# Raw blocks of the seven-product units side by side, x statistics partly on ScalarE, two more gate/up units made in the first quarter and down's weights later

## The chip, the cores and the metric

One NeuronCore of a Trainium2 chip runs the kernel. TensorE (PE) multiplies, VectorE (DVE), ScalarE (ACT) and GpSimd (POOL) work elementwise, and SyncE (SP) issues the DMAs, one after the other in program order. Every engine has its own queue and takes its instructions in order; an instruction whose semaphore has not come holds up all that is queued behind it on that engine. The metric is device time in microseconds (us), median of three runs.

## The reference

A block of two layers over x (2048 rows, 448 columns), each with a residual: a Fourier mixing and a gated feed-forward. All weights and transform matrices are inputs.

```python
x = A_x
h  = x + A(layernorm(x))      # a = xn @ Wd_re.T, b = xn @ Wd_im.T ; y = Ws_re @ a - Ws_im @ b
h2 = h + B(layernorm(h))      # g = hn @ w_gate, u = hn @ w_up ; (gelu(g) * u) @ w_down
# Ws: 2048 x 2048 (re, im); Wd: 448 x 448 (re, im); w_gate, w_up: 448 x 1792; w_down: 1792 x 448
```

The layer norms have no scale or shift, the gelu is the tanh approximation, and everything is float32.

## The kernel before

**Precision.** Every float32 operand is split into a high f16 part (ACT, `hi_part`, L105) and a low f16 part (DVE, `lo_part`, L108), and every product is made of three matmuls: high by high and the two cross terms.

**The transform (to about 347 us).** An F slot computes the features a and b of one tile of 128 rows; a U slot ("unit") multiplies one block of the sequence matrix with the features of a pair of tiles. Eight passes of eight units make h, 256 rows a pass; passes accumulate in four PSUM banks. Three units are plain (24 matmuls), and five, `S_UNITS`, use a scheme of seven half products (42 matmuls of half the width). Such a unit needs, besides raw blocks of its weights (`wr`), four sums of them (`seq_sums`, L515, on DVE), all split into high and low; of the four raw blocks it uses three, which are numbers 0, 2 and 3, in two instructions per engine (`seq_parts`, L525). The features of such a tile get sums too (`feature_sums`). At the same time the other engines make ready what comes later: the statistics and the norm of the next x tiles, the layer norm of finished passes, their splitting into operands of the feed-forward part and the DMA transposes of these (`ffn_sums`, `ffn_hi`, `ffn_lo`, `ffn_transpose`), and the weights of 11 of the 14 gate/up units, which are summed, split and stored to DRAM (`Weights.high`, `Weights.low`). The order of all this on each queue is made by a planner (`arranged`, L928) when the program is built: tasks with a cost, a due time and predecessors, taken by due time per engine. Due times carry an offset by kind (`SHIFT`). The order before it, from L980 to L1036, is written out by hand.

**The feed-forward part.** Four quarters of 512 rows in operands, 14 gate/up units each (t = 0 to 55; loop at L1439). A gate/up unit has seven products, 39 matmuls on three PSUM banks X, Y and Z. In the code they are `x_open`, `x_close`, `y_open`, `y_mid`, `y_close`, `z_open` and `z_close`; the part called hh is read out of Z and Y by DVE (L1209, L1266) with help of ACT (`u2`, `u3`, the gelu), and POOL multiplies its last block (`c_last`). `y_mid`'s read of Z must be over before `z_close` adds to the bank. From t = 14 on each unit is followed by 21 matmuls of the down projection for the hidden rows made earlier (`dn_mm`), with down chunk n = d mod 7 of the weights, d = t - 14.

**The first quarter (t = 0 to 13)** has no down matmuls. In it are made

- the gate/up units in `LATE` (4, 8, 12), from raw weights in the order of beats, two to a unit t (`late_prep(2 * t)` after `y_mid`, `late_prep(2 * t + 1)` at the end); a beat issues sums, high parts and low parts; one raw tile is loaded (`gu_late`) as soon as the one before is read;
- down's seven weight chunks (`down_load`, `down_sums` on POOL, `down_hi`, `down_lo`, driven by `down_prep(t - 1)`): chunk n belongs to t = 2n + 1 and 2n + 2; its raw tile `wd32` takes one of two buffers in turn, and two chunks are loaded ahead, the first already in the transform.

Work beside the units, such as the norm and splitting of pass pairs for quarters 2 and 3 and the drains of down, hangs in a table `side` and is issued by `do(t, k)` at place k of unit t; within a unit of quarters 1 to 3 the places come in the order 0, 6, 1, 4, 5, 2, 3, 7, and in quarter 0 there are none.

Of the kernel before, what the change touches and what calls it, by code (L numbers as in the profile page):

```python
# [33 lines left out]
def kernel(  # L34
# [57 lines left out]
    G.memset(eps_t, EPS / X_SC**2)  # L92

# [115 lines left out]
    def ffn_root(q, j):  # L209
        moments[q, j] = moments[q, j], root(moments[q, j], f"h{q}_{j}", moments_of(q, j))  # L210

    def ffn_rstd_steps(q, j):
        mv, sd = moments[q, j]
        found = []
        steps = rstd_steps(found, mv, sd, f"h{q}_{j}", const, moments_of(q, j))
        next(steps)
        moments[q, j] = mv, found[0]
        yield
        yield from steps
# [8 lines left out]
    def down_load(n):  # L228
        wd32[n] = fops.tile([P, 4, HD], F32, tag="tt" if n % 2 else "xn", name=f"wd32_{n}")
        nc.sync.dma_start(wd32[n].rearrange("p (k c) d -> p k (c d)", k=2), w_down[n])  # L230
# [91 lines left out]
    S_UNITS, WR_BUFS, WS_BUFS, WSS_BUFS, STAGE_BUFS = (3, 4, 5, 6, 7), 3, 3, 2, 2  # L322
    ORDER = (0, 1, 5, 2, 6, 3, 7, 4)
# [4 lines left out]
    xt, xs, xT, norm_x = {}, {}, {}, {}  # L328
    x_pairs = x.rearrange("(u g p) d -> u p g d", g=2, p=P)
# [27 lines left out]

    def x_root(*tiles):
        norm_x[tiles] = norm_x[tiles], root(norm_x[tiles], f"x{tiles[0]}")

    def x_rstd_steps(*tiles):
        mv, sd = norm_x.pop(tiles)
        found = []
        steps = rstd_steps(found, mv, sd, f"x{tiles[0]}")
# [10 lines left out]
    def x_bias(*tiles):  # L375
        mv, r, _ = norm_x[tiles[0]]
        nb = small.tile([P, len(tiles)], F32, tag=f"nb{len(tiles)}", name=f"nb_x{tiles[0]}")
        bias_of(nb, mv, r)
        for i in tiles:
            norm_x[i] += (nb,)  # L380
# [134 lines left out]
    def seq_sums(p, u):  # L515
        r = wr[p, u]
        s = wsum[p, u] = dft.tile([P, 4, 2 * P], F32, tag="wsum", bufs=1, name=f"wsum{p}_{u}")
        V.tensor_add(s[:, 0:2], r[:, 1:2].to_broadcast([P, 2, 2 * P]), r[:, 0:4:3])
        yield
        V.tensor_add(s[:, 2], s[:, 1], r[:, 0])  # L520
        yield
        V.tensor_add(s[:, 3], s[:, 2], r[:, 2])  # L522
# [39 lines left out]
    PRODUCTS = [(0, 0, 2, 0), (1, 2, 0, 1), (6, 1, 0, 0), (2, 6, 1, 1), (4, 3, 2, 1), (5, 5, 3, 0), (3, 4, 3, 1)]  # L562
# [42 lines left out]
    def seq_out(p):  # L605
# [12 lines left out]
        for g, ps in enumerate((X, Y)):  # L618
            eg = e[:, 2 * g : 2 * g + 2].rearrange("p o d -> p (o d)")
# [10 lines left out]
    class Weights:  # L630
# [52 lines left out]
        def beat(self, k):  # L683
# [19 lines left out]
    for k, u in enumerate(ORDER):  # L703
        slots += [("F", i) for i in tiles_of[k]]
        due = [v for v in ready if not is_s(v) or ORDER.index(v) < k - 1]
        if k:
            slots += [("U", 0, v) for v in due[:1]]
            ready = [v for v in ready if v not in due[:1]]
# [22 lines left out]
    class Task:  # L731
# [5 lines left out]
    SHIFT = {"copy": -31.8, "fhigh": -68.2, "fhighp": -18.1, "flow": 9.9, "fsum": 12.9, "guhi": 1.2, "gulo":  # L737
        22.8, "guraw": -33.2, "gus1": -3.2, "gus2": 31.0, "hbias": -61.6, "hhi": -17.7, "hlo": 16.0,
        "hnorm": -24.0, "hroot": 35.4, "hrstd": 5.9, "hsum": 23.1, "htr": 140.0, "mom": 32.7, "out": -5.4,
        "seed": -14.0, "shigh": -55.6, "slow": 3.4, "whigh": -12.1, "whigh_s": -34.3, "wload": -73.7,  # L740
        "wlow": 2.9, "wlow_s": -3.8, "wsum": -12.5, "xbias": 12.2, "xlo": 1.3, "xnorm": 26.7, "xroot": -6.1,
        "xrstd": 21.6, "xstat": 21.3, "xturn": -1.8}
    HOLD = (0.23, 17.8)
# [6 lines left out]
    def add(*args, **kw):  # L750
        tasks.append(Task(*args, **kw))
        return tasks[-1]

    def chain(engine, costs, due, make, after=(), kind=None):
# [8 lines left out]
        for k, cost in enumerate(costs):  # L763
            last = [add(engine, cost, due, lambda k=k: step(k == 0), after=last, kind=kind)]
# [14 lines left out]
    for k, (i, i2) in enumerate(tiles_of):  # L779
        n = where["F", i]  # L780
        if k > 1:
# [4 lines left out]
            t = add("V", 1.35, T[max(n - 6, 0)] + first_pair, lambda i=i, j=i2: x_stats(i, j), begin=T[max(n - 7, 0)] - 13.0, after=[t], kind="xstat" if k > 2 else None)  # L786
            t = add("A", 0.3, T[max(n - 5, 0)] + first_pair, lambda i=i, j=i2: x_root(i, j), after=[t], kind="xroot" if k > 2 else None)
            t = chain("V", (0.2, 0.1, 0.1, 0.1), T[max(n - 5, 0)] + first_pair, lambda i=i, j=i2: x_rstd_steps(i, j), [t], kind="xrstd" if k > 2 else None)
            t = add("V", 0.15, T[max(n - 5, 0)] + first_pair, lambda i=i, j=i2: x_bias(i, j), after=[t], kind="xbias" if k > 2 else None)
            for c in (i, i2):  # L790
                n = where["F", c]
                low = fixed(n - 5, 5, "A", 1.15, lambda i=c: x_norm(i), [t], kind="xnorm")
                low = fixed(n - 5, 5, "V", 0.85, lambda i=c: x_lo(i), [low], kind="xlo")
                turned[c] = fixed(n - 4, 2, "SP", 1.3, lambda i=c: x_turn(i), [low], lag=2.6, kind="xturn")
                steps[n].after += [turned[c]]
        for c in (i, i2):
# [8 lines left out]
            else:  # L805
# [4 lines left out]
                t = drained = add("V", 1.07, T[n + 1] + 2.5 if n > 1 else -30.0 + n, lambda i=c: feature_low(i), after=[t], kind="flow" if n > 1 else None)  # L810
# [15 lines left out]
    for g, (p, u) in enumerate(units):  # L826
# [23 lines left out]
    at_end = T[len(slots)]  # L850
    h_done, rooms, last_e = {}, {}, []
    for p in range(N_PASS):
# [15 lines left out]
        t = add("A", 0.25, t0 + 14.0, lambda q=q, j=j: ffn_root(q, j), after=m, kind="hroot")  # L868
        t = chain("V", (0.2, 0.1, 0.1, 0.1), t0 + 15.0, lambda q=q, j=j: ffn_rstd_steps(q, j), [t], kind="hrstd")
        last_e, h_done[p] = m, [store, t]  # L870
        if q < 2:
            t = add("V", 0.15, t0 + 16.0, lambda q=q, j=j: ffn_bias(q, j), after=[t], kind="hbias")
            t = add("A", 1.35, t0 + 17.0, lambda q=q, j=j: ffn_norm_act(q, j, hp[q, j]), after=[t], kind="hnorm")
            h_done[p] = [store, t]
            for k in range(4):
# [12 lines left out]
    LATE = {4: 0, 8: 7, 12: 15}  # L888
# [35 lines left out]
    t = fixed(len(slots) - 14, 9, "SP", 0.1, lambda: down_load(0), last_e, lag=6.0, kind="dload")  # L924
    fixed(len(slots) - 8, 9, "G", 4.0, lambda: down_sums(0), [t], kind="dsum")
# [115 lines left out]
    for _, t in arranged():  # L1041
# [10 lines left out]
        if t == p1_end:  # L1052
            first.close()
# [31 lines left out]
    down_load(1)  # L1085
# [83 lines left out]
    def down_prep(t):  # L1169

        n, odd = divmod(t, 2)
        if odd:
            if n < NC:
                down_lo(n, 1)
                if n + 2 < NC:
                    down_load(n + 2)
            if n + 1 < NC:
                down_sums(n + 1)
        elif n < NC:
            down_hi(n, 0)  # L1180
            down_lo(n, 0)

# [142 lines left out]
    def dn_drain(p):  # L1325
        v = [ftile(f"v{k}", 1, f"v{k}_{p}", D) for k in range(2)]
# [37 lines left out]
    for q in (2, 3):  # L1364
# [53 lines left out]
    late_beats = {n + k: (f, k) for f, n in LATE.items() for k in range(6)}  # L1418
    assert len(late_beats) == 6 * len(LATE)

    def late_prep(beat):
        if beat not in late_beats:
            return
        f, k = late_beats[beat]
        gu[f].beat(k)
        after = [v for v in LATE if v > f]
        if k == 3 and after:
            gu_late(after[0])
        if k == 5:
            gw[f] = gu[f].w  # L1430
# [8 lines left out]
    for t in range(N_GU):  # L1439
# [12 lines left out]
        if d >= 0 and d % NC == 1:  # L1452
# [4 lines left out]
        if q == 0:  # L1457
# [8 lines left out]
            if t > 0 and t % 2 == 0 and t < 2 * NC:  # L1466
                down_hi(t // 2 - 1, 1)
# [5 lines left out]
            if t > 0:  # L1473
                down_prep(t - 1)
            late_prep(2 * t + 1)
        else:
# [80 lines left out]
    assert not side  # L1557
# [59 lines left out]
```

## Time and profile before

| what | value |
|---|---|
| median of 3 runs | 707.02 us (705.33 to 707.19) |
| profiled execution: span, first to last instruction | 703.5 us |
| mean granted clock of TensorE | 0.999 |
| transform | to about 347.4 us |
| first quarter | about 347.5 to 409 us |
| quarters 1 to 3 and the end | 409 to 703.5 us |
| PE, DVE, ACT, POOL busy | 697.0, 563.2, 408.0, 198.8 us |
| DMA, 16 engines | 139.74 MB, mean 199 GB/s |

The times of the table's stages are read off the timeline of PE, where the instructions change from one line of the kernel to another. Busy time of an engine is the union of its instructions; a PE instruction overlaps its neighbours, so the mean duration of a matmul is longer than the distance to the next. Where a view of the profile names a releaser, it is the event that ended an idle stretch.

### The profile page before, as it was taken

The page shows a single profiled execution, that of the slowest core. Times are in us where ns is not written, and L with a number is a line of the kernel's source. Part 1 is how long each engine was busy: PE and PEld are TensorE (multiplying, and loading weights), DVE is VectorE, ACT ScalarE, POOL GpSimd, SP SyncE. Part 2 cuts the span into 40 slices and gives each one's busy share as a digit, 9 for nine tenths or more (in the row PEclk, how much of TensorE's full clock was granted, in tenths as well). Part 3 has the DMA queues.
Part 4 walks back from the last instruction along what each step waited for, and adds up shares of the span by engine and source line. Part 5 has one row for each costly group of instructions (what it writes and reads, how often), then busy time and mean ns, then how long its engine had stood idle before and what let it go on. Part 6 is the DMA issues. An engine that isn't in the chain of part 4 may idle for free.

```text
span 703.5 us, 15378 instructions
## 1 busy us (share of the span) xinstructions
PE 697.0 (99%) x6046; PEld 584.1 (83%) x6046; DVE 563.2 (80%) x1170; ACT 408.0 (58%) x862; POOL 198.8 (28%) x225
## 2 busy tenths in 40 slices
PE   8999999999999999999999999999999999999998
PEld 5556578878787878778888889999999999999998
DVE  6999999999999897989578877575765755786786
ACT  5776674667576565656267765555555544455432
POOL 0000000000000000001136754474664745647342
PEclk9999999999999999999999999999999999999999
DMA  9554555687988867777579665658466594545401
GB/s 330 160 128 114 142 170 184 233 245 227 228 275 202 283 177 261 262 253 281 182 258 353 204 211 170 191 180 199 170 195 190 178 200 173 181 158 166 151 27 54
DMA packets 81849, 139.74 MB, mean 199 GB/s; under 512 B 41712, under 2 KB 59376, under 8 KB 81776
## 3 DMA queue, kind: packets, MB, share of 16 engines
q1 hardware_dynamic: 81776, 138.76, 63.5%
q8 instruction: 47, 0.77, 0.5%
q14 instruction: 26, 0.21, 0.1%
HBM read 109.25 MB, written 20.19 MB: 184 GB/s over the span
## 4 chain that ended last, share of the span: by engine, by line
PE 95%; DMA 1%; ACT 1%; DVE 1%; issue 1%; SPq 0%; ACTq 0%; DVEq 0%
PE acc L574 38%; PE acc_d L1144 15%; PE pY L1199 14%; PE pZ L1199 9%; PE pX L1199 9%; PE ab L457 9%; DMA x<-in_x_dram 1%; DVE dn_w L110 0%; ACT dn_w L106 0%; SPq L429 0%; ACT xn_h L254 0%; DVE st_x L354 0%; DVE hh L1209 0%; ACT wd L106 0%; ACT g L1252 0%
## 5 line engine op out<-in xcount | busy, mean ns | idle before, releaser
L1199 PEld LDWEIGHTS <-gw 128*128 128x128 f16 x2184 | 213.1, 98 | 23.7 <-issue 1.0
L574 PE MATMUL acc<-b,ws 128*128 128x224 f16 (+1 forms) x1296 | 204.6, 301 | 0.0
L574 PEld LDWEIGHTS <-ws 128*128 128x128 f16 x1296 | 125.6, 98 | 53.2
L1199 PE MATMUL pY<-hops,gw 128*128 128x256 f16 x952 | 129.1, 273 | 0.0
L1144 PE MATMUL acc_d<-wd,dn_w 128*128 128x224 f16 x1050 | 122.3, 259 | 0.0
L574 PE MATMUL acc<-b,wss 128*128 128x224 f16 x960 | 118.2, 259 | 0.0
L235 POOL TENSOR_TENSOR wd_s<-wd 128x448 f32<-128x448 f32 x7 | 10.1, 1442 | 346.8 <-DMA wr<-in_w_seq_dram 330.0
L1144 PEld LDWEIGHTS <-dn_w 128*128 128x128 f16 x1050 | 101.1, 98 | 2.9
L574 PEld LDWEIGHTS <-wss 128*128 128x128 f16 x960 | 92.3, 98 | 0.1
L106 ACT ACTIVATE ws<-wr 128x256 f16<-128x256 f32 (+2 forms) x104 | 62.4, 637 | 41.1 <-PE acc L574 16.1
L1199 PE MATMUL pZ<-hops,gw 128*128 128x256 f16 x616 | 85.5, 273 | 0.4 <-DVE hh L1209 0.3
L1276 POOL TENSOR_TENSOR hh<-hh,c 128x256 f32<-128x256 f32 x56 | 46.3, 828 | 139.7 <-ACT c L1274 139.5
L1199 PE MATMUL pX<-hops,gw 128*128 128x256 f16 x616 | 83.3, 273 | 0.0
L112 DVE SCALAR_TENSOR_TENSOR ws<-wr,ws 128x256 f16<-128x256 f32 (+2 forms) x104 | 70.6, 709 | 1.4 <-ACT ws L106 1.3
L110 DVE TENSOR_TENSOR dn_w<-hh,dn_w 128x256 f16<-128x256 f32 x50 | 25.3, 506 | 53.1 <-ACT dn_w L106 52.8
L106 ACT ACTIVATE wss<-wsum 128x1024 f16<-128x1024 f32 x40 | 42.1, 1053 | 36.8 <-DVE wsum L522 21.1
L457 PEld LDWEIGHTS <-xT 128*128 128x128 f16 x352 | 33.9, 98 | 32.8 <-ACT xT L420 1.5
L110 DVE TENSOR_TENSOR dn_w<-dn_s,dn_w 128x640 f16<-128x640 f32 x50 | 54.6, 1092 | 7.4 <-ACT dn_w L106 6.7
L1243 ACT ACTIVATE u<-pY 128x256 f32<-128x256 f32 x56 | 21.4, 382 | 61.4 <-PE pY L1199 61.3
L1291 POOL TENSOR_TENSOR dn_s<-hh 128x256 f32<-128x256 f32 x42 | 52.8, 1258 | 0.0
L112 DVE SCALAR_TENSOR_TENSOR wss<-wsum,wss 128x1024 f16<-128x1024 f32 x40 | 48.8, 1220 | 4.1 <-ACT wss L106 4.0
L1238 ACT ACTIVATE pY<-pX 128x256 f32<-128x256 f32 x56 | 20.6, 368 | 50.3 <-PE pX L1199 50.3
(120 smaller groups left out, 936.9 us busy)
## 6 DMA issues: line engine op xcount, KB each, us to landing
gw<-w_dram SPq DMA_DIRECT2D x53, 896.0 KB, 4.8
wr<-in_w_seq_dram SPq DMA_DIRECT2D x64, 512.0 KB, 4.4
gu_raw<-in_w_gu_dram SPq DMA_DIRECT2D x28, 384.0 KB, 4.8
w_dram<-gu_p SPq DMA_DIRECT2D x33, 256.0 KB, 3.1
hx<-in_x_dram SPq DMA_DIRECT2D x8, 448.0 KB, 4.5
h_dram<-hx SPq DMA_DIRECT2D x8, 448.0 KB, 4.8
hr<-h_dram SPq DMA_DIRECT2D x8, 448.0 KB, 5.3
x<-in_x_dram SPq DMA_DIRECT2D x7, 448.0 KB, 6.9
```

Of the source, the lines that this page charges most:

```text
L106: A.activation(dst, src, AF.Copy, scale=scale)
L110: V.tensor_sub(dst, src, hi)
L112: V.scalar_tensor_tensor(dst, src, scale, hi, op0=ALU.mult, op1=ALU.subtract)
L235: G.tensor_sub(s[:, 2:4], t[:, 0:2], t[:, 2:4])
L457: PE.matmul(feat[i][r][:, :D], xT[i][:, kx, :], w[:, kw, r * D : (r + 1) * D], start=n == 0, stop=n == 10,)
L574: PE.matmul(banks[k][:, cols], lhs, rhs, start=k not in begun, stop=stop, skip_group_check=True)
L1144: PE.matmul(acc[k // 2][:, k % 2 * HD : (k % 2 + 1) * HD], a_of(la, a), b_of(lb, b), start=first and m == 0 and k % 2 == 0, stop=last and ...
L1199: PE.matmul(ps, w[:, wl, wa + ws, :], ops[:, m + ms, :], start=first and n == 0, stop=last and n == len(terms) - 1, skip_group_check=True,)
L1238: A.activation(self.Y, self.X, AF.Copy)
L1243: A.activation(self.u2, self.Y, AF.Copy, scale=SC)
L1276: G.tensor_mul(c22, c22, self.c12)
L1291: E.tensor_sub(s[:, 2:4], t[:, 1:4:2], t[:, 0:4:2])
```

## The change

- *Raw blocks*: the seven-product scheme is rewritten with rows exchanged, so that it uses raw blocks 1, 2 and 3, which lie side by side; one instruction per engine splits them where there were two. `PRODUCTS` and the read-out (`seq_out`) exchange the banks accordingly.
- *Statistics*: for the x pairs 7 and 4 the sums are made by ACT (two passes with accumulation) and no longer by DVE. Where ACT makes the sums, for x or for h, two small steps of the reciprocal root go to ACT as well.
- *Slots*: a plain unit follows its features at once, a seven-product unit one pair later than before; `SHIFT` and `HOLD` have new values.
- *First quarter*: `LATE` has five units; beats are five to a unit instead of six and follow one another from 0 to 23; a raw tile is asked for at the third beat. The splitting and transposes of pass 3 (second quarter's operands) leave the transform for t = 0 to 4.
- *Down's weights*: chunk n belongs to t = 6 + 2n and 7 + 2n, to t = 19; `wd32` has one buffer (tag v, which the drains use later), loaded one chunk ahead at the end of t = 6 + 2n; the first load and its sums are at the end of t = 4 and t = 5, behind the transposes. `down_hi` of the sums goes to `down_mid`.
- *Quarter 2's splitting* is five and eight units later, but its first norm stays at t = 14; one load of h for a drain is three units later.
- SBUF: the last b tile takes the place of an x tile, so that the first pool lives to the end of the transform.

The diff, cut to its core:

```diff
+    def half_of(mv, tag, pool=small, of=1):
+        n = mv.shape[1]
+        r = pool.tile([P, 4, n], F32, tag=f"r{n}" if pool is small else f"r_{tag}", name=f"r_{tag}")
+        A.activation(r[:, 1], mv[:, :, 1], AF.Identity, scale=-0.5 / (of * X_SC**2), bias=half_eps)
+        return r
...
-        V.tensor_mul(r[:, 2], r[:, 0], r[:, 0])
+        if by_vector:
+            V.tensor_mul(r[:, 2], r[:, 0], r[:, 0])
+        else:
+            A.activation(r[:, 2], r[:, 0], AF.Square)
...
     def down_load(n):
-        wd32[n] = fops.tile([P, 4, HD], F32, tag="tt" if n % 2 else "xn", name=f"wd32_{n}")
+        wd32[n] = fpool.tile([P, 4, HD], F32, tag="v", name=f"wd32_{n}")
...
+    BY_SCALAR = (7, 4)
+    HALF, BEHIND = {}, 0
...
+    def x_moments(i, tiles):
+        if i == tiles[0]:
+            norm_x[tiles] = small.tile([P, 2, 2], F32, tag="mv2", name=f"mv_x{i}")
+        act_moments(norm_x[tiles][:, tiles.index(i), :], xt[i][0], junk)
...
-        V.tensor_add(s[:, 0:2], r[:, 1:2].to_broadcast([P, 2, 2 * P]), r[:, 0:4:3])
+        V.tensor_add(s[:, 0:2], r[:, 0:1].to_broadcast([P, 2, 2 * P]), r[:, 1:3])
...
-            return [(w[0], slice(0, 1), r[:, 0:1]), (w[0], slice(1, 3), r[:, 2:4])]
+            return [(w[0], slice(0, 3), r[:, 1:4])]
...
-            if k > 1:
-                s0, s1, src = parts[k - 2]
+            for n in ((), (), (0, 1), (2,), (3,))[k]:
+                s0, s1, src = parts[n]
                 lo_part(self.slots(1, s0, s1, src), src, self.slots(0, s0, s1, src), W_SC)
-            if 0 < k < 5:
-                s0, s1, src = parts[k - 1]
+            for n in ((), (0, 1), (2,), (3,), ())[k]:
+                s0, s1, src = parts[n]
                 hi_part(self.slots(0, s0, s1, src), src, W_SC)
...
+            if i % 2 == HALF.get(k, 1):
+                due = [v for v in ready if ORDER.index(v) < k - (2 if is_s(v) else BEHIND)]
...
-    LATE = {4: 0, 8: 7, 12: 15}
+    LATE = {4: 0, 6: 5, 9: 10, 11: 15, 13: 19}
...
-    t = fixed(len(slots) - 14, 9, "SP", 0.1, lambda: down_load(0), last_e, lag=6.0, kind="dload")
-    fixed(len(slots) - 8, 9, "G", 4.0, lambda: down_sums(0), [t], kind="dsum")
...
         n, odd = divmod(t, 2)
         if odd:
-            if n < NC:
+            if 0 <= n < NC:
                 down_lo(n, 1)
-                if n + 2 < NC:
-                    down_load(n + 2)
-            if n + 1 < NC:
+            if n + 1 < NC and n >= 0:
                 down_sums(n + 1)
-        elif n < NC:
+        elif 0 <= n < NC:
             down_hi(n, 0)
             down_lo(n, 0)
+            if n + 1 < NC:
+                down_load(n + 1)
+
+    WD0 = 6
+
+    def down_mid(t):
+        n, odd = divmod(t - WD0, 2)
+        if odd and 0 <= n < NC:
+            down_hi(n, 1)
...
+        (4, 4, lambda: ffn_transpose(1, 1, (2,))),
+        (4, 4, lambda: ffn_transpose(1, 1, (3,))),
+        (4, 4, lambda: down_load(0)),
+        (5, 4, lambda: down_sums(0)),
...
+            if k == 2 and after:
+                gu_late(after[0])
...
             late_prep(2 * t)
...
+            do(t, 1)
+            down_mid(t)
             nxt.z_open()
             nxt.y_open()
             cur.y_close()
             cur.z_close()
             dn_ahead(t)
-            if t > 0:
-                down_prep(t - 1)
+            do(t, 2)
+            down_prep(t - WD0)
             late_prep(2 * t + 1)
+            do(t, 4)
         else:
...
             if nxt:
                 nxt.y_open()
-            if t == 2 * NC:
-                down_hi(NC - 1, 1)
-            if t == 2 * NC + 1:
-                down_lo(NC - 1, 1)
+            down_mid(t)
+            down_prep(t - WD0)
             do(t, 2)
```

More of the change, by code (lines that the diff above doesn't have):

```diff
@@ L92 @@
     G.memset(eps_t, EPS / X_SC**2)
+    half_eps = const.tile([P, 1], F32, name="half_eps")
+    G.memset(half_eps, -0.5 * EPS / X_SC**2)
     warm = const.tile([P, 1], F32, name="warm")
@@ L328 @@
     xt, xs, xT, norm_x = {}, {}, {}, {}
+    by_scalar = tuple((2 * u, 2 * u + 1) for u in BY_SCALAR)
+    junk = p1.tile([P, D], F16, name="junk")
     x_pairs = x.rearrange("(u g p) d -> u p g d", g=2, p=P)
@@ L356, in x_stats, with x_of @@
             V.bn_aggr(mv[:, g, :], st)
+    def x_moments(i, tiles):
+        if i == tiles[0]:
+            norm_x[tiles] = small.tile([P, 2, 2], F32, tag="mv2", name=f"mv_x{i}")
+        act_moments(norm_x[tiles][:, tiles.index(i), :], xt[i][0], junk)
+    def x_of(tiles):
+        return D if tiles in by_scalar else 1
     def x_root(*tiles):
-        norm_x[tiles] = norm_x[tiles], root(norm_x[tiles], f"x{tiles[0]}")
+        mv, of, tag = norm_x[tiles], x_of(tiles), f"x{tiles[0]}"
+        r = half_of(mv, tag, small, of) if of > 1 else None
+        norm_x[tiles] = mv, root(mv, tag, of), r
     def x_rstd_steps(*tiles):
-        mv, sd = norm_x.pop(tiles)
+        mv, sd, r = norm_x.pop(tiles)
         found = []
-        steps = rstd_steps(found, mv, sd, f"x{tiles[0]}")
+        steps = rstd_steps(found, mv, sd, f"x{tiles[0]}", of=x_of(tiles), r=r)
         next(steps)
@@ L501, in sums_high @@
     def sums_high(i):
-        t = bop[i] = dft.tile([P, 2, 7, HD], F16, name=f"b{i}")
+        if i == tiles_of[-1][1]:
+            t = p1.tile([P, 2, 7, HD], F16, tag="xs", name=f"b{i}")
+        else:
+            t = dft.tile([P, 2, 7, HD], F16, name=f"b{i}")
+        bop[i] = t
         hi_part(t[:, 0], b32[i][:, 1:8])
@@ L703 @@
     for k, u in enumerate(ORDER):
[L704 to L708, printed above, removed]
+        for i in tiles_of[k]:
+            slots.append(("F", i))
+            if i % 2 == HALF.get(k, 1):
+                due = [v for v in ready if ORDER.index(v) < k - (2 if is_s(v) else BEHIND)]
+                slots += [("U", 0, v) for v in due[:1]]
+                ready = [v for v in ready if v not in due[:1]]
         ready.append(u)
@@ L763, in chain @@
         for k, cost in enumerate(costs):
-            last = [add(engine, cost, due, lambda k=k: step(k == 0), after=last, kind=kind)]
+            on, cost = cost if isinstance(cost, tuple) else (engine, cost)
+            last = [add(on, cost, due, lambda k=k: step(k == 0), after=last, kind=kind)]
         return last[0]
@@ L1084 @@
     h_store(N_PASS - 1)
-    down_load(1)
     banks_dft.close()
@@ L1325, in dn_drain @@
     def dn_drain(p):
-        v = [ftile(f"v{k}", 1, f"v{k}_{p}", D) for k in range(2)]
+        v = fpool.tile([P, 2, D], F32, tag="v", name=f"v_{p}")
+        v = [v[:, k] for k in range(2)]
         return Drain(hr[p], acc_d[p], v, 1.0 / (H_SC * W_SC))
@@ L1416 @@
     odd_q = None
-    late_beats = {n + k: (f, k) for f, n in LATE.items() for k in range(6)}
-    assert len(late_beats) == 6 * len(LATE)
+    late_beats = {}
+    for f, n in LATE.items():
+        for k in range(5):
+            at(late_beats, n + k, (f, k))
     def late_prep(beat):
[L1422 to L1430, printed above, removed]
+        for f, k in late_beats.pop(beat, ()):
+            gu[f].beat(k)
+            after = [v for v in LATE if v > f]
+            if k == 2 and after:
+                gu_late(after[0])
+            if k == 4:
+                gw[f] = gu[f].w
     cur = GateUp(0)
@@ L1556 @@
     part_store(7, 1, 1)
-    assert not side
+    assert not side and not late_beats
 def _tiles(inputs):
```

122 lines of the change are left out of this document (86 added, 36 removed).

## The prediction, made before the changed kernel was run

> **What bounds the kernel now.** I read the page first, then the chain of waits in order of time, then the first quarter of the feed-forward part unit by unit.
>
> ```profile
> span 703.5 us, 15378 instructions
> PE 697.0 (99%) x6046; PEld 584.1 (83%) x6046; DVE 563.2 (80%) x1170; ACT 408.0 (58%) x862; POOL 198.8 (28%) x225
> PE 95%; DMA 1%; ACT 1%; DVE 1%; issue 1%; SPq 0%; ACTq 0%; DVEq 0%
> ```
>
> A busy PE need not be at its peak, so I compare lengths in the chain (start, us, what) with counts.
>
> ```profile
> 13.37 2.44 PE ab L457 x12
> ...
> 27.77 4.54 PE acc L574 x24
> ...
> 61.82 4.03 PE acc L574 x42
> ...
> 99.38 248.30 PE acc L574 x2100
> 349.65 1.20 PE pX L1199 x11
> ...
> 672.09 28.19 PE acc_d L1144 x294
> ```
>
> A plain unit takes 4.54, a seven-product unit 4.03. The 2100 matmuls are 21 plain and 38 seven-product units: 95.3 + 153.1 = 248.5 us, and the row has 248.30. So the transform has no stall there. In the feed-forward part a gate/up matmul takes 1.20/11 = 0.109 and a down matmul 28.19/294 = 0.0959; 2184 and 1176 of them make 351.1 us. They fill 347.5 (the first gate/up matmul, 2.1 before the 349.65 row) to 672.09 + 28.19 = 700.3, which is 352.8. **All the stalls that could be won back behind 13.4 us are some 1.7 us, 0.24%.** One of them has this row:
>
> ```profile
> 420.12 0.71 PE L1199 MATMUL pZ<-hops,gw 128*128 128x256 f16 x5 [0.29 <-DVE hh L1209]
> ```
>
> Before 13.4 us the order is written out by hand, and the change leaves it alone; the tail after 700.3 too.
>
> **The change part by part, at the profiled execution's own 703.5.** The median of the runs, 707.02, is 3.5 above this span; I put that on top of the new sum.
>
> The transform first (the grouped view of 100 to 340 us, and of the whole).
>
> ```profile
> L112 DVE SCALAR_TENSOR_TENSOR ws<-wr,ws 128x512 f16<-128x512 f32 x36 | 24.6, 684 | 0.1
> L112 DVE SCALAR_TENSOR_TENSOR ws<-wr,ws 128x256 f16<-128x256 f32 x36 | 15.0, 418 | 0.3 <-ACT ws L106 0.3
> L106 ACT ACTIVATE xs<-tt 128x768 f16<-128x768 f32 x4 | 3.3, 827 | 0.0
> L354 DVE BATCH_NORM_STATS2 st_x<-x 128x6 f32<-128x448 f32 x16 | 9.2, 613 | 4.3 <-DMA x<-in_x_dram 4.3
> L128 ACT ACTIVATE e<-hx,mv_h 128x448 f32<-128x448 f32 x14 | 9.4, 669 | 0.5
> ```
>
> *Raw blocks side by side*: 40 times, DVE's 684 + 418 ns become one operation of 768 columns, bounded by 684 and 1102; by length 0.95. That is some 6 us less for DVE; ACT's one is near the 827. *Statistics*: four tiles of x lose about 0.8 each on DVE (613 and its aggregate) and gain about 1.8 each on ACT (two passes like the 669, with accumulator reads). The two small steps that each root now gives to ACT are under 0.5 us nine times. *Two gate/up units and one pass's splitting leave the transform*: DVE loses some 4.4 and 5 us apiece. All of it is worth **zero to the end**, since PE runs without a gap over this work; were the cover gone, DVE's relief, some 25 us in 330, could count. *The new slot order* keeps the same matmuls; it puts four F slots in a row at units 7 and 4. Bounds: 0, and a rival below. I take 0, by the 248.30 row.
>
> Now the first quarter (units t = 0 to 13). What matters there is PE, unit 4 here, and what DVE had:
>
> ```profile
> 366.69 1.36 PE L1199 MATMUL pX<-hops,gw 128*128 128x256 f16 x11
> ...
> 370.41 0.71 PE L1199 MATMUL pZ<-hops,gw 128*128 128x256 f16 x5
> 370.95 1.36 PE L1199 MATMUL pX<-hops,gw 128*128 128x256 f16 x11
> ```
>
> A unit lasts 4.26, so unit 10 starts at 392.2. Its z_close is 3.72 in (the pZ row), at 395.9, and cannot start until DVE's hh of that unit has read the Z bank; hh is queued behind all that DVE was given before.
>
> **The step that I expect to cost: a chain through one buffer.** The old kernel had two buffers for down's raw weights; the new one has one (tag v), and reads of it on POOL (down_sums), ACT and DVE must be over before the next load. SP issues in order, so what stands behind a waiting load waits too. Both are in the old trace:
>
> ```profile
> 376.01 1.04 POOL L238 TENSOR_TENSOR wd_s<-wd 128x224 f32<-128x224 f32 x1
> ```
> ```profile
> 375.12 0.81 SPq L637 DMA_DIRECT2D gu_raw<-in_w_gu_dram  x2
> ...
> 377.08 0.33 SPq L230 DMA_DIRECT2D wd<-in_w_down_dram  x1
> ...
> 389.36 7.66 SPq L1073 DMA_DIRECT2D gw<-w_dram  x2
> ```
>
> The load at 377.08 went when POOL's sums ended at 377.05; at 389.36 SP stood still until a tile came free. The terms (the tile views of wd, of gu_raw, both 340 to 430 us, and the line of the transposes; ns min/median/max):
>
> ```profile
> L106 ACT ACTIVATE wd<-wd_s x7: 1125/1127/1129, 361.1 to 416.0; 128x1120 f16<-128x1120 f32 x7
> L112 DVE SCALAR_TENSOR_TENSOR wd<-wd_s,wd x7: 1308/1315/1319, 363.0 to 421.4; 128x1120 f16<-128x1120 f32 x7
> L235 POOL TENSOR_TENSOR wd_s<-wd x6: 1127/1326/1518, 364.4 to 408.1; 128x448 f32<-128x448 f32 x6
> L237 POOL TENSOR_TENSOR wd_s<-wd x6: 1128/1136/1313, 365.9 to 409.2; 128x448 f32<-128x448 f32 x6
> L238 POOL TENSOR_TENSOR wd_s<-wd x6: 651/654/1048, 367.0 to 410.3; 128x224 f32<-128x224 f32 x6
> DMA to landing us min/median/max: 4.0/5.5/7.0
> ```
> ```profile
> L112 DVE SCALAR_TENSOR_TENSOR gw<-gu_raw,gw x6: 420/684/1023, 356.8 to 390.9; 128x512 f16<-128x512 f32 x3, 128x256 f16<-128x256 f32 x3
> L643 DVE TENSOR_TENSOR gu_s<-gu_raw x3: 544/548/1079, 352.8 to 385.4; 128x384 f32<-128x384 f32 x3
> DMA to landing us min/median/max: 3.1/5.0/5.9
> ```
> ```profile
> L315 SPq DMA_TRANSPOSE hops<-xs x32: 1183/1297/3398, 152.2 to 573.3; - x32
> ```
>
> Five gate/up units now share beats 0 to 23, two to a unit, and the raw tile of the next is asked for at the third beat. For unit 9 that is the end of t = 3: DVE starts there at about 367.0 (z_close of t = 3 ends as 366.69 begins), does c, a small split and two low parts (0.34 + 0.2 + 0.95), so SP issues the two loads at 368.5. Behind them on SP: those loads 0.8, two transposes 2.6, a gate/up load and a store 0.7, two transposes 2.6; down_load(0) goes at **375.2** and lands 5.5 later, 380.7. POOL sums it, 1.33 + 1.14 + 0.65 = 3.1: 383.8. Only then may down_load(1) go: lands 389.3, summed 392.4. down_load(2) goes then (0.33), and *behind it on SP* stand the two raw loads for unit 13 (second issue at 393.2): landed 398.2. DVE has the first sums of unit 13 in its queue at the end of t = 9, so it stands until 398.2, does them (0.55 + 0.3) and hh (0.42): 399.5. PE's z_close of unit 10, due at 395.9, is **3.6 us late**. On the way ACT waits for chunk 0 at the end of t = 6 and for chunk 1 at the end of t = 8, with the next unit's gelu and its copy of X into Y queued behind, and PE's y_open behind that copy. Those stalls, under 1 each, are inside the 3.6, for the chain runs through absolute times. With every minimum (4.0, 2.9, 4.0, 2.9, 3.1) unit 13's weights land at 392.9, before DVE needs them: 0. With every maximum the lateness is near 9. I take the medians, since the DMA engines are nearly full already in 362 to 389 us (packets, MB, share of 16 engines), and the change brings two gate/up loads and stores more into the quarter:
>
> ```profile
> q1 hardware_dynamic: 2004, 9.38, 94.8%
> ```
>
> The splitting of pass 3, now in t = 0 to 4, gives DVE some 0.7 a unit where down's parts (1.8 a pair of units) stood before: 0. What later weights wait for is then covered, since quarter 1's units last longer (below, 6.27).
>
> **A second one, at t = 20.** The last chunk's high and low parts are issued at the end of t = 19, behind y_open; dn_mm of t = 20 is the first to read them, in its second product term. The same place in the old trace:
>
> ```profile
> 446.03 0.82 PE L1199 MATMUL pY<-hops,gw 128*128 128x256 f16 x6
> 446.89 0.38 ACT L1243 ACTIVATE u<-pY 128x256 f32<-128x256 f32 x1 [1.67 <-PE pY L1199]
> 447.89 0.93 PE L1144 MATMUL acc_d<-wd,dn_w 128*128 128x224 f16 x8
> ```
>
> ACT's u ends its turn at 447.2, the high part takes 1.13 (448.3), DVE's low part 1.32 (449.6). PE wants it at 447.99: **1.7 us late**, bounds 1.4 and 2.0 by handover. No later work gives that back, PE having no slack.
>
> **A small gain**: the stall at t = 15 comes with the old last chunk beside ffn_norm_act; a smaller piece of chunk 4 stands there now. Its size:
>
> ```profile
> 416.08 0.93 PE L1144 MATMUL acc_d<-wd,dn_w 128*128 128x224 f16 x8
> ...
> 422.81 0.93 PE L1144 MATMUL acc_d<-wd,dn_w 128*128 128x224 f16 x8
> ```
>
> The two units stand 6.73 apart, and 21 x 0.0959 + 39 x 0.109 is 6.27: 0.46. Bounds -0.46 and +0.5, I take -0.4. hr_load(1), three units later, still has two units before its drain: 0.
>
> Sum: 3.6 + 1.7 - 0.4 = +4.9; span 708.4, **711.9** as a time.
>
> **The rivals.**
> *A, the chain hides* (not slower): the loads land as fast as their minima, 4.0 and 3.1, so unit 13's weights are there before DVE asks. It decides at about 3.6 us less over the three landings. For it: those minima occur. Against: the 94.8%. Left is 1.7 - 0.4: 708.3, +0.2%, inside the 0.3% (2.1 us) that a measurement of this kernel tells from no change.
> *B, a net gain*: also t = 20 is covered and the small stalls shrink, up to -1.7: about 706. Against it stands the order of ACT's queue.
> *C, DVE becomes the bound of the first quarter*, without a late load. For it (windows, PE, PEld, DVE, ACT, POOL busy):
>
> ```profile
> 366.68:370.94 4.26, 4.26 (x41) 3.81 (x40) 4.04 (x8) 3.20 (x8) 2.94 (x4) 1.00 0.97 297
> 370.94:375.20 4.26, 4.26 (x41) 3.82 (x40) 4.26 (x8) 3.23 (x10) 1.94 (x2) 1.00 0.77 282
> ```
>
> There one gate/up unit was made over three units; now it is over two and a half, in units 6 to 11 beside down's parts. At some 4.4 of DVE each (four sums up to 0.55, four low parts up to 0.68) that adds 0.3 to 4.1: 4.4 against 4.26, six times, 0.9: with t = 20, 709.2. PE kept its pace in those rows, which speaks against more. If each POOL sum (3.1) instead shut DVE out for its whole length, 1.6 a unit with t = 6 to 11 would cost up to 6 more, some 714. [...]
> *D, the new transform order stalls PE*: an S tile's sums and low part hold DVE some 3.2, and with four F slots in a row one may come late; +3.2 on the forecast, 715.1. For it: DVE is 9 tenths busy there. Against: 25 us less for DVE.
>
> **How the numbers follow.** Forecast 0.50, A 0.22, B 0.08, C 0.08, D 0.12. C's 0.08 holds 0.02 for the full lock. Slower by over 0.3% (above 709.1): forecast nearly all (0.47), D 0.12, C 0.06, A's upper edge 0.05: 0.70. Faster (below 704.9): half of B, 0.04. Same: 0.26. Range 706.5 to 716.0: it leaves out B's lower half and the chain's longest landings with D.
>
> **What would show it.** In the profile after: POOL's wd_s waiting on wd's DMA (never more than hidden before); DVE's gu_s near 395 to 398 waiting on gu_raw; PE pZ waiting on hh there; PE acc_d waiting on DVE wd about 447 plus the delay. In the chain the acc row of the transform keeps about 4.03 and 4.54 a unit. It is wrong if gu_raw lands before DVE asks, if PE acc_d at t = 20 waits under 1 us, or if PE shows gaps in the transform.

## Result and profile after

The changed kernel takes 736.51 us (median of 4 runs, 733.59 to 738.04); the kernel before took 706.35 us (4 runs, 705.33 to 707.19) beside it. The ratio is 1.0426, 95% interval 1.0400 to 1.0452. I had predicted 711.9: slower was right, but 30 us were lost where I had summed 5. One run of all that follow, in experiment 8, took 1489.04 us and is left out of its ratio. From the page of the profile after:

```profile
span 734.4 us, 15278 instructions
PE 704.9 (96%) x6046; PEld 587.1 (80%) x6046; DVE 561.0 (76%) x1104; ACT 413.0 (56%) x860; POOL 195.6 (27%) x226
PE 86%; DMA 5%; DVE 4%; ACT 3%; POOL 1%; issue 1%; SPq 1%; DVEq 0%; ACTq 0%
```

DVE has less to do than before (561.0 against 563.2) and the kernel is slower. The chain of waits, which was PE to 95%, now holds 5% DMA. Its longest piece is the transform:

```profile
95.40 252.31 PE acc L610 x2142
```

2142 matmuls are one seven-product unit more than the 2100 of before, 248.30 + 4.03 = 252.33. So the transform has no stall, as forecast, and the loss lies behind it. What PE waited for from 340 us on (us in total, times, longest):

```profile
PE pZ L1254 <- DVE hh L1264: 14.0, 8, 7.2
PE pY L1254 <- ACT pY L1293: 7.5, 1, 7.5
PE acc_d L1191 <- DVE wd L114: 1.1, 1, 1.1
...
```

With two more of 0.3 that is 23.2 us where the kernel before had 0.3. The span grew by 30.9, so some 8 us are not idle time at all. The chain in order of time over the first quarter (start, us, what) shows both:

```profile
375.90 8.10 DMA w_dram<-gw
...
384.55 0.40 ACT gw L108
385.55 2.50 PE pY L1254 x11
...
389.12 2.29 PE pX L1254 x11
...
392.72 1.20 PE pY L1254 x11
...
403.27 6.79 DMA gu_raw<-in_w_gu_dram
...
413.27 2.17 PE pX L1254 x11
...
427.33 10.82 DMA w_dram<-gw
438.35 0.44 DVE hh L1264
438.83 1.23 PE pZ L1254 x5
```

Three transfers stand in it. Two are *write-backs* of late units' finished weights, which I had given no price: at 375.90 (unit 4) and 427.33 (unit 13). The third is the raw load of unit 13, which I had expected, at about its place.

**Why a write-back can stop PE.** A late unit's finished weights stay in SBUF for their own use and are also copied to DRAM for the later quarters. The copy is issued when the unit is used, so unit 4's goes in t = 4. The next writer of the same place stood until it had landed. Unit 9 takes the place of unit 4 (both have f % 5 = 4), and its first high part is made at the end of t = 5. The row on ACT:

```profile
384.02 0.94 ACT L108 ACTIVATE gw<-gu_raw 128x512 f16<-128x512 f32 x2 [9.28 <-DMA w_dram<-gw]
```

ACT stood 9.28 us with the gelu and the copy of X into Y queued behind, and PE's pY behind that copy. Unit 13's place (f % 5 = 3) lies in the scratch pool that is closed at t = 14, where the hidden values hh of quarter 1 then lie: DVE's first hh of t = 14 stood 7.82 us for the write-back of t = 13. In the old kernel, with the late units 4, 8 and 12, the next writer of such a place was always a load (unit 9's into unit 4's place), and SP's queue took the wait (340 to 430 us; us in total, times, longest):

```profile
SPq L1073 <- DMA w_dram<-gw: 16.1, 3, 8.2
```

There it held up only later loads, and PE stood 0.3 us in all from 340 us on. In the change the next writer is ACT for unit 4's place and DVE for unit 13's, and PE waits for both. The trace before thus already showed the wait, only on a queue with room to spare.

**The slow groups.** In the chain a group of 11 matmuls takes 1.20 us, but 2.50, 2.29 and 2.17 behind the stalls. Windows of the same stretch (busy time of PE, PEld, DVE, ACT, POOL, then the granted clock, the DMA share and GB/s):

```profile
378.00:380.00 2.00, 0.03 (x1) 0.00 (x0) 0.09 (x1) 0.00 (x0) 0.00 (x0) 1.00 0.97 276
380.00:382.00 2.00, 0.00 (x0) 0.00 (x0) 0.00 (x0) 0.00 (x0) 0.00 (x0) 0.75 0.97 394
382.00:384.00 2.00, 0.00 (x0) 0.00 (x0) 0.00 (x0) 0.00 (x0) 0.00 (x0) 0.50 1.07 260
...
390.00:392.00 2.00, 2.00 (x14) 1.54 (x13) 1.62 (x2) 0.93 (x3) 2.00 (x3) 0.69 0.97 314
```

PE stopped at 378.0. The clock fell to a half at 381 and came back at about 391.2 (0.69 in the window from 390), though PE worked again from 385.55: 5.7 us at half speed, some 2.8 lost beyond the idle time.

### The profile page after: what moved, and what is told of

It is laid out like the page before. It is cut to its first block, busy times and chain, and to the rows that moved or that the text cites. A ratio compares the mean times of both kernels' runs of the same rounds, so it can differ in the third digit from the quotient of the medians.

```text
span 734.4 us, 15278 instructions
## 1 busy us (share of the span) xinstructions
PE 704.9 (96%) x6046; PEld 587.1 (80%) x6046; DVE 561.0 (76%) x1104; ACT 413.0 (56%) x860; POOL 195.6 (27%) x226
## 4 chain that ended last, share of the span: by engine, by line
PE 86%; DMA 5%; DVE 4%; ACT 3%; POOL 1%; issue 1%; SPq 1%; DVEq 0%; ACTq 0%
PE acc L610 36%; PE acc_d L1191 14%; PE pY L1254 12%; PE pZ L1254 8%; PE ab L489 8%; PE pX L1254 8%; DMA w_dram<-gw 3%; DVE dn_w L112 1%; DMA x<-in_x_dram 1%; DMA gu_raw<-in_w_gu_dram 1%; DVE wd L114 1%; DMA xT<-xs 1%; ACT b L108 0%; ACT wd L108 0%; DVE hh L1264 0%
## 5 line engine op out<-in xcount | busy, mean ns | idle before, releaser
L1254 PEld LDWEIGHTS <-gw 128*128 128x128 f16 x2184 | 216.2, 99 | 49.4 <-issue 24.1
L1254 PE MATMUL pY<-hops,gw 128*128 128x256 f16 x952 | 130.9, 275 | 7.8 <-ACT pY L1293 7.5
L1254 PE MATMUL pZ<-hops,gw 128*128 128x256 f16 x616 | 87.1, 276 | 14.1 <-DVE hh L1264 14.0
L108 ACT ACTIVATE ws<-wr 128x1024 f16<-128x1024 f32 (+1 forms) x64 | 58.7, 920 | 62.5 <-PE acc L610 50.0
L1254 PE MATMUL pX<-hops,gw 128*128 128x256 f16 x616 | 85.8, 278 | 0.0
L114 DVE SCALAR_TENSOR_TENSOR ws<-wr,ws 128x1024 f16<-128x1024 f32 (+1 forms) x64 | 67.0, 1053 | 10.7 <-ACT ws L108 10.7
L489 PE MATMUL ab<-wh_hi,xT 128*128 128x448 f16 x224 | 45.6, 353 | 1.2 <-ACT wh_hi L108 0.4
```

The source lines that it names most:

```text
L108: A.activation(dst, src, AF.Copy, scale=scale)
L114: V.scalar_tensor_tensor(dst, src, scale, hi, op0=ALU.mult, op1=ALU.subtract)
L489: PE.matmul(feat[i][r][:, :D], xT[i][:, kx, :], w[:, kw, r * D : (r + 1) * D], start=n == 0, stop=n == 10,)
L1254: PE.matmul(ps, w[:, wl, wa + ws, :], ops[:, m + ms, :], start=first and n == 0, stop=last and n == len(terms) - 1, skip_group_check=True,)
```

## The experiments

Theory 1: the two write-backs and unit 13's raw tile are the loss, each with a slow stretch behind it. Against it stood my prediction (loads through down's one raw buffer) and its rival C (DVE, slowed by POOL).

**1 to 3: write back early.** Each finished unit is copied to DRAM at its last beat: only unit 4, only unit 13 (the others as in the change), or all five:

```diff
             if k == 4:
                 gw[f] = gu[f].w
+                gu[f].store()
...
-            if t in LATE:
-                gu[t].store()
```

> Unit 4's finished weights are written back at the end of t = 2 (its last beat, beat 4) instead of in the middle of t = 4; nothing else is moved. Theory 1 (unit 9's high part must wait until the write-back that reads the same place has landed, and PE is slow for some us after it has stood): the 7.5 us before pY at 385.6 go, and so does what the two groups after it lost (2.50 and 2.29 where 1.20 is usual, 2.4 in all), so some 9.3 us, the whole excess of unit 6 over 4.26: 736.5 - 9.3 = 727.2. Theory 2 (only the idle time counts, the slow groups are something else): 736.5 - 7.5 = 729.0. Rival (the chain of loads through down's one raw buffer, which I predicted, runs through absolute times): units 7 to 10 come earlier, the raw loads of unit 13 do not, and the stall at pZ grows from 4.4 to some 12: nothing won, 735 to 737.

Measured 730.67 us, ratio 1.0343 (1.0316 to 1.0370): 5.8 less than the changed kernel, where theory 1 said 9.3 and the chain of loads that I had predicted said nothing.

> Unit 13's weights are written back at the end of t = 11 instead of in the middle of t = 13; nothing else is moved. Theory 1 (the hidden values of quarter 1 lie where unit 13's weights lay, so DVE's first hh of t = 14 waits until the write-back has landed; then PE is slow for some us): the 7.2 idle us at 438.8 go and the slow groups after them, 9.1 less 0.3 in all: 727.5. Idle time only: 729.3. Rival (DVE is behind by as much at t = 14 from the quarter before, and the write-back only ends at about the same time): less than 2 us, 735 or more.

Measured 727.65, ratio 1.0302 (1.0269 to 1.0335): 8.9 less, and theory 1 said 9.0.

> All five late units are written back at the beat in which they are finished (four of them two, one a unit and a half earlier than before). Theory 1: the two stalls add: 736.5 - 9.3 - 8.8 = 718.4, and the stall at unit 13's raw weights, 4.4 idle, remains. Idle time only: 721.8. Rival (chain of loads in absolute times): the first comes back at pZ of unit 10 or 11: 727 to 729.

Measured 723.52, ratio 1.0244 (1.0222 to 1.0266): 13.0 less, where 18.1 were expected. So the write-backs are 13 of the 30 us, and the rest of what the first one had cost came back as another wait. Rows of ACT and the sum of PE's waits for it, in the kernel with all five early:

```profile
386.20 0.58 ACT L108 ACTIVATE wd<-wd 128x448 f16<-128x448 f32 x1 [7.21 <-DMA wd<-in_w_down_dram]
```
```profile
PE pY L1254 <- ACT pY L1293: 4.1, 1, 4.1
```

The same copy now waits behind the high part of down's first chunk, because that chunk's load has not landed. This is the side stall of my prediction ("ACT waits for chunk 0 at the end of t = 6 with the next unit's gelu and its copy of X into Y queued behind"), put there at under 1 us. Why it is late shows on SP, here in the changed kernel itself:

```profile
369.05 0.80 SPq L673 DMA_DIRECT2D gu_raw<-in_w_gu_dram  x2
369.89 5.33 SPq L332 DMA_TRANSPOSE hops<-xs  x2
375.32 0.53 SPq L1121 DMA_DIRECT2D gw<-w_dram  x1
375.90 0.42 SPq L734 DMA_DIRECT2D w_dram<-gw  x1
376.36 4.78 SPq L332 DMA_TRANSPOSE hops<-xs  x2
381.19 0.59 SPq L247 DMA_DIRECT2D wd<-in_w_down_dram  x1
```

Two transposes hold SP 4.8 to 5.3 us; I had 2.6, from the median over the whole kernel before. The load of the first chunk went at 381.19, not 375.2, and the write-back of unit 4 stood in the same queue.

**4: a second raw tile**, on top of the early write-backs.

```diff
-            self.raw = pool.tile([P, 2, 6, P], F32, tag="raw", name=f"gu_raw{f}")
+            self.raw = pool.tile([P, 2, 6, P], F32, tag="raw", bufs=1 if pool is p2 else 2, name=f"gu_raw{f}")
```

> As the kernel with all five write-backs early, and the raw gate/up weights of the late units have two buffers in turn instead of one. Theory 1 (the raw loads of unit 13 go out late because DVE must first have read unit 11's raw tile for the last time): pZ's 4.4 us of idle time at 412 go with the slow groups after it, 5 of unit 10's excess: 713.4. Rival (my prediction: the raw loads stand on SP behind a load of down's weights that waits for POOL's sums): they still stand there, 718.4 as without the second buffer. Rival 2 (DVE is too full in t = 6 to 11, whatever lands): 1 to 2 won at most, 716.5 to 718.4.

Measured 717.55, ratio 1.0153 (1.0132 to 1.0174): 6.0 less than without it. In the changed kernel two waits stood one behind the other on SP. The load of down's third chunk, issued just ahead of unit 13's raw loads, stood 5.3 us until DVE's low part of the chunk before was done (401.38; POOL's sums were over at 399.91) and went at 401.46. The raw load went at 402.89, 1.4 later, when DVE had read unit 11's raw tile for the last time (402.86). With two raw tiles it still goes right behind a load of down's weights (394.77 and 394.39), so what the raw tile alone is worth stays open. Part of the 6.0 is another stall: raw loads that leave earlier also let the transposes go earlier (at 367.29 and 373.02, where they had gone at 369.91 and 375.92), and pY's stall fell from 4.1 to 1.4.

**5 and 6: down's loads.** First chunk's load ahead of the transposes; then a second buffer for every other chunk.

```diff
-        (4, 4, lambda: down_load(0)),
+        (2, 4, lambda: down_load(0)),
...
-        wd32[n] = fpool.tile([P, 4, HD], F32, tag="v", name=f"wd32_{n}")
+        wd32[n] = (fops if n % 2 else fpool).tile([P, 4, HD], F32, tag="tt" if n % 2 else "v", name=f"wd32_{n}")
```

> The kernel with all write-backs early and two raw buffers (717.55), and in addition the load of down's first chunk goes to SP at the end of t = 2, ahead of the four transposes of t = 3 and 4, instead of behind them at the end of t = 4. Theory (with the first write-back out of the way, ACT's high part of that chunk is next to hold up the copy of X into Y, because two transposes took 3.7 and 5.0 us on SP where I had 2.6): pY's 1.36 and pZ's 0.71 at 383.5 to 385.6 go, with the slow groups after them some 2.5: 715.0. Rival (the DMA engines are full there, and the earlier load only makes the raw weights of unit 9 and 6 land later): nothing won, 717 to 719.

Measured 716.60, ratio 1.0157 (1.0131 to 1.0184): within the uncertainty of the run without it. The load was in time, but the two stalls became one of 2.1 us in pY, behind ACT's high part of that chunk's sums, which POOL began at 382.4. These sums are written where the last pass's split values were, which the transposes read. In experiment 6 the same operation's wait ends with a transpose (hops<-xs):

```profile
383.33 1.13 POOL L252 TENSOR_TENSOR wd_s<-wd 128x448 f32<-128x448 f32 x1 [9.64 <-DMA hops<-xs]
```

But the trace of experiment 5 itself puts the end of that wait down to DVE's hh, and no run moved the transposes, so that they held the sums is argued and not shown.

> As the kernel with the early first load, and every second chunk of down's raw weights goes to a second buffer, so that no load waits for POOL's sums of the chunk before. My prediction (the chain load, sums, load through one buffer sets unit 10 and 11): the two stalls at pZ left there, 1.71 and 1.34, go: 3 less than the kernel with the early first load, 712. Rival (the loads are in time by then, and DVE is slowed by POOL working beside it: its 417 ns operation took 1346 there): the same within 1 us, 714 to 715.5.

Measured 717.00, ratio 1.0152 (1.0133 to 1.0171): no difference, although unit 13's raw loads now went at 386.57, where they had gone at 393.58 in experiment 5. With two raw tiles the chain through one buffer, the main term of my sum, is worth nothing. Alone on the changed kernel the second buffer was not tried.

**7: no sums on POOL.**

```diff
     def down_sums(n):
+        if n:
+            wd_s[n] = wd_s[0]
+            return
```

> As the kernel with the second buffer for down's raw weights, but POOL's sums of chunks 1 to 6 are left out (each chunk is given the sums of chunk 0, so six sevenths of down's summed weights are not computed); DVE and ACT split as many elements as before. Rival C of the prediction (POOL's sums slow DVE's operations beside them): DVE's groups keep their 417, 681, 1020 ns, the two stalls of 1.71 and 1.34 go, 709 to 712.5. Otherwise (DVE has simply too many operations in t = 6 to 11, or loads are late): less than 1 us won over the kernel with the second buffer.

This kernel leaves out the sums of six chunks of seven; it only serves to see what they cost. Measured 713.43, ratio 1.0106 (1.0084 to 1.0129): 3.6 less, just outside the 709 to 712.5, but far from "less than 1". DVE's operations on unit 13's raw tile, with the sums beside them (first fence) and without:

```profile
399.03 1.38 DVE L679 TENSOR_TENSOR gu_s<-gu_raw 128x384 f32<-128x384 f32 x1
400.33 1.34 DVE L680 TENSOR_TENSOR gu_s<-gu_raw 128x256 f32<-128x256 f32 x1
...
405.35 2.08 DVE L114 SCALAR_TENSOR_TENSOR gw<-gu_raw,gw 128x512 f16<-128x512 f32 x2
```
```profile
397.58 0.72 DVE L682 TENSOR_TENSOR gu_s<-gu_raw 128x384 f32<-128x384 f32 x1 [0.28 <-DMA gu_raw<-in_w_gu_dram]
398.23 0.95 DVE L683 TENSOR_TENSOR gu_s<-gu_raw 128x256 f32<-128x256 f32 x1
...
401.95 1.55 DVE L114 SCALAR_TENSOR_TENSOR gw<-gu_raw,gw 128x512 f16<-128x512 f32 x2
```

POOL worked at its sums from 398.47 to 402.2 in the first. Undisturbed, the middle one takes 0.42, as the tile view of the changed kernel has it (ns, min/median/max):

```profile
L680 DVE TENSOR_TENSOR gu_s<-gu_raw x5: 419/420/1357, 353.3 to 410.7; 128x256 f32<-128x256 f32 x5
```

In the kernel without the sums POOL still adds up hidden values beside these two operations (397.85 to 399.76), which fits the 0.72 and 0.95. With the sums, the operations of 1.38 and 1.34 began beside a POOL sum that was already running and ended at 400.41 and 401.67, 0.3 to 0.4 us behind the end of that sum (399.99 and 401.39). How the two engines hinder each other no run shows beyond that.

**8: the raw blocks alone**, in the kernel before (its seven-product sums, parts and product list changed as in the change, and nothing else).

> The kernel before with one part of the change: the raw blocks of the seven-product units side by side, so that DVE's 36 pairs of 684 and 418 ns become single operations of 768 columns; order, write-backs and down's loads are those of before. My prediction (PE has no gap over that work): 0, 705.4 to 706.8. Rival (DVE's relief counts in the transform's end or the first quarter): up to 0.3 less at the one stall there is, below 705.8; a longer operation that delays hh behind it: up to 0.5 more.

Measured 705.96 (median of all ten runs) against 706.02, ratio 1.0002 (0.9989 to 1.0014). Nothing, as forecast.

**9 and 10: what a stall costs.** The kernel before, with idle work for DVE at t = 40, for one chunk or for three:

```diff
+    idle_out = const.tile([P, 1], F32, name="idle_out")
...
+            if t == 40:
+                for n in range(1):
+                    V.reduce_sum(idle_out, wd[:, n].rearrange("p l o d -> p (l o d)"), axis=mybir.AxisListType.X)
             cur.y_mid()
```

> The kernel before, with one more piece of work for DVE: in the middle of t = 40, ahead of y_mid's hh, it sums the 3136 columns of one chunk of down's split weights into a tile nobody reads (at 1.31 us for 1120 columns some 3.3 to 3.7 us). DVE's hh is normally done 1.1 us ahead of pZ, so PE stands some 2.2 to 2.6 us, once. Theory (PE's clock is only lowered after some 3 us of standing): the loss is the idle time, 708.2 to 708.6. Rival (any stall of that size is followed by slow groups): 710 or more. Rival 2 (the slack takes it in): 706.1.

Measured 709.53, ratio 1.0056 (1.0039 to 1.0074).

> The same with three chunks, 9408 columns, some 10 to 11 us of DVE: PE stands 8.8 to 10 us once. Theory (after some 3 us without work the granted clock goes to a half and comes back only after some 5 us of work, so a long stall costs 2.5 to 3 more than it lasts): 706.1 + 8.8 to 10 + 2.5 to 3 = 717.4 to 719.1. Rival (a stall costs what it lasts): 714.9 to 716.1.

Measured 718.50, ratio 1.0173 (1.0152 to 1.0195). PE's rows about the stall, in the kernel before, the short stall and the long:

```profile
576.60 0.71 PE L1199 MATMUL pY<-hops,gw 128*128 128x256 f16 x5
...
586.10 0.93 PE L1144 MATMUL acc_d<-wd,dn_w 128*128 128x224 f16 x8
```
```profile
577.25 0.71 PE L1199 MATMUL pY<-hops,gw 128*128 128x256 f16 x5
579.97 0.71 PE L1199 MATMUL pZ<-hops,gw 128*128 128x256 f16 x5 [2.01 <-DVE hh L1209]
...
590.59 0.93 PE L1144 MATMUL acc_d<-wd,dn_w 128*128 128x224 f16 x8
```
```profile
578.42 0.71 PE L1199 MATMUL pY<-hops,gw 128*128 128x256 f16 x5
588.05 1.22 PE L1199 MATMUL pZ<-hops,gw 128*128 128x256 f16 x5 [8.92 <-DVE hh L1209]
...
599.26 0.93 PE L1144 MATMUL acc_d<-wd,dn_w 128*128 128x224 f16 x8
```

From pY to the acc_d behind it the kernel before takes 9.50 us and the short stall 13.34: 3.84 lost for 2.01 idle. So a stall of 2 us can cost twice its length; my theory that PE must stand for 3 us first (3.0 in the changed kernel, 378.0 to 381) fell. It does not always: the mean clock was 0.997 in two of the four runs (709.8 and 710.91 us) and 1.000 in the other two (709.25 and 708.12). For the long one the same acc_d starts at 599.26, 20.84 behind its pY: 11.34 lost for 8.92. The price beyond the idle time is 1.8 and 2.4, nearly the same. By the medians the two kernels lose 3.9 and 12.9 us; the profiled execution of the long one is 1.8 us late ahead of the stall already, which is not explained.

**11 and 12: down's parts laid elsewhere**, on the kernel of experiment 6 (first and second parts at the end of the units named in the expectations).

> The kernel with early write-backs, two raw buffers, the early first load and two buffers for down's raw weights (717.0), and the last chunk's first parts are made at the end of t = 17 and its last parts at the end of t = 18, one unit earlier each. My prediction's second step (PE stands at t = 20 for that chunk, 0.3 and 1.1 in that kernel): these 1.4 go, and DVE has 0.6 more in t = 17 and 1.3 more in t = 18, up to 0.5 back: 715.6 to 716.1. Rival (the stall at pZ of t = 18 and 19 grows by what was won): 717.0.

Measured 717.40, ratio 1.0176 (1.0158 to 1.0193). The 1.4 at t = 20 went, and a stall of 1.89 came at pZ of t = 18: nothing won.

> The same kernel with down's chunks laid elsewhere: first parts and POOL's sums at the end of t = 7, 11, 13, 14, 15, 16, 17, second parts at the end of t = 9, 13, 14, 15, 16, 17, 18, so that POOL makes no such sums in t = 8 to 10, where five late units still keep DVE busy, and the first sums do not wait for the last transposes of pass 3. Theory (POOL's sums beside a full DVE, and the first chunk behind the transposes, are what is left of the first quarter's loss): pY's 2.7, the two stalls at pZ of 1.7 and 1.3 and the 1.4 at t = 20 go; quarter 1's units take 1 us of DVE more each in t = 14 to 18, up to 0.6 a unit lost there: 717.0 - 7.1 + 3 = 712.9, bounds 710 and 715. Rival (the late units alone are too much for DVE): 715.5 to 717.

Measured 721.83, ratio 1.0232 (1.0216 to 1.0247): 4.8 slower, outside the bounds given. PE's waits, and DVE's rows ahead of one of these stalls, in t = 16:

```profile
PE pZ L1253 <- DVE hh L1263: 13.9, 10, 2.2
```
```profile
432.92 1.35 DVE L112 TENSOR_TENSOR dn_w<-hh,dn_w 128x256 f16<-128x256 f32 x1
434.20 1.75 DVE L112 TENSOR_TENSOR dn_w<-dn_s,dn_w 128x640 f16<-128x640 f32 x1
```

Parts of two chunks at the end of one unit of quarter 1 cost PE 1.89 us in the next, since they and the split of dn_w stand ahead of hh. That split took 1.35 and 1.75, where the medians of the kernel before are 0.45 and 1.09; that POOL slowed it, busy 6.00 of the 8.30 us from 428.7 to 437, is my reading and not shown. The "up to 0.6 a unit" was too small, and neither of the two other places tried for down's parts won anything.

## Why the prediction was wrong in size

- **The step that failed** is the first quarter's: "Five gate/up units now share beats 0 to 23", after which I priced only what these beats compute and load. I did not ask where each finished tile lies, who writes that place next and when its copy to DRAM lands. Instead, a write-back was waited for by ACT (9.28 us) and one by DVE (7.82), and PE stood 7.5 and 7.2 us behind them. Putting the copies earlier won 13.0 us; together with the second raw tile, 19.0 of the 30.
- **"A chain through one buffer"** named the right stall, pZ of unit 10 (4.38 us idle, predicted 3.6), for a reason that was right in part only. SP did stand at a load of down's weights, to 401.46, but for DVE's low part of the chunk before, not for POOL's sums, and the one raw tile then held the raw load to 402.89. DVE was late there with everything behind the first stall; by these rows it was not the landing times that I had added up, and a second buffer for down's chunks, beside a second raw tile, changed nothing. The size was luck.
- **SP's transposes** were mis-sized: 2.6 for two, measured 4.8 to 5.3, so the first load left 6.0 late. In the changed kernel this was hidden behind the first write-back.
- **t = 20**: 1.7 predicted, bounds 1.4 and 2.0; the rows have 0.30 + 1.10 = 1.4. Right.

```profile
460.19 0.71 PE L1254 MATMUL pZ<-hops,gw 128*128 128x256 f16 x5 [0.64 <-DVE hh L1264]
467.04 0.71 PE L1254 MATMUL pZ<-hops,gw 128*128 128x256 f16 x5 [0.42 <-DVE hh L1264]
476.45 0.26 PE L1191 MATMUL acc_d<-wd,dn_w 128*128 128x224 f16 x1 [0.30 <-ACT wd L108]
477.81 0.83 PE L1191 MATMUL acc_d<-wd,dn_w 128*128 128x224 f16 x7 [1.10 <-DVE wd L114]
```

- **The small gain** of 0.4 at t = 15 came, but t = 17 and 18 lost 0.64 and 0.42 (the first two rows above), to which I had given no term.
- **The transform at 0**: right, by its one chain row and by experiment 8. Rival D did not occur.
- **Rival C**, DVE as the bound, got 0.08 and is much of what is left once the transfers are out of the way: leaving POOL's sums out won 3.6, and the two new places for down's parts cost as much as they won or more. A full lock, 0.02 of the 0.08, no run shows: in experiment 6 DVE ended operations at 400.41 and 401.67, while POOL's sums went on to 402.2. The kernel before says nothing on it: DVE's 1120-column operation (1308 to 1319 ns) never ran beside POOL's sums there, most of which begin when it ends (POOL's idle time before them: us in total, times, longest):

```profile
POOL wd_s L235 <- DVE wd L112: 13.6, 5, 3.5
```

- **A term that was missing**: the clock. I priced stalls at their length. The half clock behind them took some 2.8, 1.5 and 1.8 us more in the changed kernel (PE was back at 385.55, 412.05 and 438.83, the clock at 391.2, 415.1 and 442.4): 6.1 of the 8 us that were not idle time. In experiments 9 and 10 it took 1.8 and 2.4.

The best of these kernels that computes everything, 716.6, is still 1.5% behind the kernel before. PE was full there to within 1.7 us, so the change had nothing to win. Of the 7.4 us that experiment 7 still loses, its trace shows 6.7 as PE's idle time; how much of it a better order could win back stays open.

## What to carry to other kernels

When a tile gets another place or time, list for its place who reads it last, *DMA reads included*, and who writes it next: a write-back that no engine waits for becomes a wait as soon as one writes the place again within its landing time (8.1 and 10.8 us for the two here). The trace before may already show such waits on SP, as here, where 16.1 us of them cost PE nothing. Price DMA issues and transfers from the rows of the stage they move into, not from the median of the kernel. And if the bound engine is full already, relief on another engine may be worth nothing (experiment 8: ratio 1.0002), while each stall costs its length and, where the clock falls, the slow stretch behind it (3.84 us for 2.01 idle, 11.34 for 8.92).

## What was new about the hardware

The granted clock fell to a half some 3.0 us after PE stopped (378.0 to 381), and in the short stall it fell *after* PE had gone back to work. From the windows of that kernel:

```profile
581.00:582.00 1.00, 1.00 (x8) 0.76 (x7) 0.14 (x1) 0.13 (x1) 0.00 (x0) 0.63 0.53 57
...
584.00:585.00 1.00, 1.00 (x9) 0.86 (x8) 0.98 (x2) 0.31 (x1) 0.91 (x2) 0.66 0.57 237
```

PE stood from 577.96 to 579.97; the half clock lasted from 581.3 to 584.7. Other stalls of that size passed without it: in experiment 12, ten stalls of up to 2.2 us, 13.9 in all, and a mean granted clock of 1.00. In the changed kernel the clock fell at 381.0, and two windows give the falls behind its other two long stalls, at 411.7 and 435.6, each 4.0 us after PE had stopped (a clock of 0.85 in a window of 1 us is a half clock for the last 0.3 us):

```profile
411.00:412.00 1.00, 0.00 (x0) 0.00 (x0) 1.00 (x3) 0.23 (x1) 0.38 (x1) 0.85 0.17 72
435.00:436.00 1.00, 0.00 (x0) 0.00 (x0) 0.00 (x0) 0.00 (x0) 1.00 (x3) 0.80 0.28 108
```

The half clock lasted 10.2, 3.4 and 6.8 us there, 10.2 in the long stall (582.5 to 592.7) and 3.4 in the short one: three, one, two, three and one times 3.4. The falls lie 30.7 and 23.9 us apart, nine and seven times the same 3.4. So the stretches and the falls measured here fit one step; what sets it, and why one stall of some 2 us is followed by the half clock and another is not, no run shows. A stall of 2.0 us was enough, though not in every run: the mean clock of the short stall's kernel was 0.997 in two and 1.000 in two.
